# Chunked attention with a Fourier-mix MLP on one core: the first batch's memory values through GpSimd's queue, a negation on VectorE, large loads first, and a cheaper extra row in a newly searched order

## The chip, the cores and the metric

The kernel runs on one core of a Trainium2 chip. A core has five engines that run in parallel, each through its own list of instructions in order: TensorE (PE; its weight loads are PEld), VectorE (DVE), ScalarE (ACT), GpSimd (POOL) and SyncE (SP), which here only issues DMAs. DMAs can be issued from SP, from ACT and from POOL. The metric is the device time of one execution in microseconds, the median over runs.

## The reference

Inputs are float32: q, k and v of 4 batches x 8 heads x 768 positions x 64, eight memory keys and values per head, and two weight matrices of 512 x 2048 and 2048 x 512. Cut to what matters:

```python
for c in range(768 // 32):                        # chunks of 32 queries
    l, r = max(0, 32*c - 16), min(768, 32*c + 40)
    k_full = concat([mem_k, k[:, :, l:r]]);  v_full = concat([mem_v, v[:, :, l:r]])
    a = softmax(q[:, :, 32*c:32*c+32] @ k_full.T / 8)
    out[:, :, 32*c:32*c+32] = a @ v_full
x = out with its heads side by side               # (4, 768, 512)
u = x + real(fft(fft(x, axis=1), axis=2))
un = (u - mean(u)) / sqrt(var(u) + 1e-6)          # over the last axis
result = u + maximum(un @ w_ch1, 0) @ w_ch2
```

## The kernel before

A batch is handled as four pairs of heads; pair n (0 to 15) lives in the buffers `qs`, `ks` (three of each) and `va` (four). For a pair, q and k are loaded as bf16 by GpSimd's queue (L383) and turned on TensorE (`trq`, `trk`, L415; the last batch by DMA instead). The 768 queries are 12 tiles of 64; a tile sees 96 keys: 8 memory keys, 16 to the left, its own 64 and 8 to the right. `va` holds for each tile the values of these 96 keys, with a column of ones beside them that gives the softmax's sum. Scores (`sc`) go through exp on ScalarE (`e`), are multiplied with `va` (`xa` for tiles 0 to 5, `xo` for 6 to 11, L523) and normalised on VectorE into `xsb` (L533, L534).

**Values.** `e_load_v` (L385 to L406) fills `va` from SP: the first tile's own 64 rows for both heads (L399), and then for each head the large load of 80 rows x 11 tiles (`run`, L392), the 8 rows to the right (L392) and the memory values (L405). In the first batch the second head's large load is issued by ScalarE instead (`half == 1`). Before the loads, `e_edges` (L353 to L355) writes the ones and clears the edges, on VectorE for `va0` and on GpSimd for the others; `e_edge_ones` (L360 to L365) corrects the ones at the edges, on GpSimd, and the first `xa` of a pair waits for that too.

**Fourier part.** The two-dimensional transform is done as matrix products with cosine and sine tables made on the chip: the angles on VectorE (L1065 to L1074), the sines on ScalarE (L1228). The first batch also needs negated copies of half of the sequence tables, `odd`, made by `e_negatives` (L1230 to L1232) on GpSimd. In the sequence direction only rows 0 to 384 are computed (`ps`, L729 for batch 0, L595 for the others); the remaining rows follow by mirror symmetry, through a round trip to DRAM (`x_rows`, `x_back`). For batches 1 to 3, `h_columns` (L789) does the same in the feature direction: per block of 128 rows it computes only the independent columns, and `h_copy`, `h_ends` and `h_mix` build the mirrored ones. Row 384 is left over from the three blocks of 128. `e_last_row` (L640 to L647) computes this extra row by six matmuls with one column of weights each, over all 256 columns of both halves (even and odd columns, `par`), into partition 0; `h_last` (L819 to L824) copies it from PSUM with two ScalarE copies, and then GpSimd may add the mirrored rows back (`h_sum_back`, L829). Mean and variance (L841), normalisation, a turn by TensorE (batch 0) or by DMA, and the MLP follow: `ph` (L906), ReLU on ScalarE (L915), then `pc` (L924 as plain products; L973 with seven products of halves for eight, on sums that VectorE makes, L961), added into `xsb` (L978).

**Order.** Nothing is scheduled by the hardware. Every step is a task of a planner (`Plan`) with an engine, an estimated cost, the tasks that it waits for and the buffers that it takes and gives. An order per engine is written out as five lists of task numbers (`lists`); the planner plays them through with its costs, and the instructions are emitted in the order that comes out. In the opening, whenever the planner's model leaves TensorE without work, it puts in dummy matmuls on a tile of zeros (`dz`, `idle`): narrow ones of 128 columns (L1046) up to 7 us of its own clock and wide ones of 512 (L1038) after that, until the first batch's Fourier data is there. They are instructions like any others: they run whether or not the real wait was as long.

A DMA signals its end on a semaphore. Eight are used in turn by the DMAs of SP and ACT, eight others by those of GpSimd, so that an issue can wait for the landing of an earlier one that used the same semaphore.

Of the kernel before, what the change touches and what calls it, by code (L numbers as in the profile page):

```python
# [14 lines left out]
ALU = mybir.AluOpType  # L15
# [193 lines left out]
def kernel(  # L209
# [176 lines left out]
    def e_load_v(n, half=None):  # L386
# [12 lines left out]
        nc.sync.dma_start(v1[OWN:OWN + 64, :, 0, 0:D],  # L399
                          v[b, 2 * pr:2 * pr + 2, 0:64].rearrange("h p d -> p h d"))  # L400
# [239 lines left out]
    def e_last_row(b):  # L640
        pm = pm_of[b, 0] if b < HALVED else pm_of[b, 0].rearrange("p (c j) -> p c j", c=2)
        for par in range(2):
            todo = [(up_of[b, par, ab][0][:, part, HS:HS + 1], (cosD, nsinD)[ab])
                    for ab in range(2 - par) for part in range(2)]
            for i, (lhs, rhs) in enumerate(todo):
                nc.tensor.matmul(pm[0:1, par, :], lhs, rhs[:, par, :], start=(i == 0),
                                 stop=(i == len(todo) - 1))  # L647
# [171 lines left out]
    def h_last(b):  # L819
        pm, full = pm_of.pop((b, 0)), full_of[b, 0][0:1]  # L820
        pl = pm[0:1].rearrange("p (c j) -> p c j", c=2)
        nc.scalar.copy(strided(full, 0, [[HD + 1, 2], [1, HD]]), pl)
        nc.scalar.copy(full[:, HD:HD + 1], pl[:, 0, 0:1])  # L823
        let_go(pm)  # L824
# [262 lines left out]
    t_used, t_val = {}, {}  # L1087

    def attention(n):
# [11 lines left out]
        if first:  # L1101
            if n % 2 == 0:
                for m in (n, n + 1):
# [4 lines left out]
        lv = add("SP", 2.7 if first else 2.5, lambda: e_load_v(n, 0 if first else None),  # L1108
                 [t_edges[n] if n < NV else None, t_used.get(("va", n % NV))] + ([t_lb[2], t_lb[3]] if n == 3 else []),
                 behind=t_x2.get(b - 2) if not first else t_lv[n - 1] if n % 2 else None if n == 0 else t_lb[n + 1],  # L1110
                 take=("va",), moved=1.65 if first else 2.7, grain=0.038, head=0.5 if first else 0.9, late=LATE,
# [44 lines left out]
        for g in range(2):  # L1156
# [39 lines left out]
            v_ = add("PE", 0.79, mode="v", emit=lambda g=g: e_values(n, g), after=[x_, lv, lb, t_ones[n]], take=(tag,),  # L1196
# [33 lines left out]
    def e_negatives():  # L1230
        for i, tab in enumerate((cosS, sinS)):
            nc.gpsimd.tensor_scalar(odd[:, i], tab[:, 1], -1.0, None, ALU.mult)  # L1232
# [24 lines left out]
    t_neg = shared(add("POOL", 3.3, e_negatives, [t_sines], rank=100))  # L1257
# [438 lines left out]
```

## Time and profile before

| what | value |
|---|---|
| time, median of 3 runs | 271.45 us (270.34 to 272.12) |
| profiled execution: span from first to last instruction | 268.6 us |
| median less that span | 2.85 us |
| TensorE busy | 262.2 us, 98% of the span |
| VectorE, ScalarE, GpSimd busy | 203.0, 161.9, 89.6 us |
| `ph` L906, 768 matmuls of 128x256 | 88.9 us |
| DMA moved | 40.00 MB, mean 149 GB/s |

The profile is of one execution. A row of the timeline reads: start, duration, engine, line, operation, output<-inputs, tile, count, and in brackets how long the engine was idle before and what released it; rows of one kind that follow each other are merged. Matmuls overlap in the pipeline, so that the time from one start to the next, and not the duration shown, is what one costs. An engine with a q behind its name is its sequencer, which issues DMAs. The waits list who waited for whom: total, times, longest. The chain of work follows back from the last instruction to what released it at each step; `...` marks lines left out.

### The profile page before, as it was taken

Reading aid. Unit: us, or ns where it says so; the run is one execution under the profiler, and the core shown is the slowest. Engines: PE = TensorE matmul, PEld = TensorE weight load, DVE = VectorE, ACT = ScalarE, POOL = GpSimd, SP = SyncE. Lnnn points to the kernel's source line nnn. Section 1 sums busy time; section 2 is a strip of 40 time slices with the busy share of each in tenths; the row PEclk is TensorE's granted clock in tenths of the full one; section 3 lists DMA queues with packets and bytes.
Section 4 is the critical chain, followed back from the end, with each engine's and each line's share of the span. In section 5 each row is a group of like instructions: output and inputs, shape, how many; then the busy total and the mean of one; then the engine's idle time right before and its main releaser. Section 6 shows DMA issues by size and latency. Waiting matters only on the chain.

```text
span 268.6 us, 8357 instructions
## 1 busy us (share of the span) xinstructions
PE 262.2 (98%) x3469; PEld 216.9 (81%) x3469; DVE 203.0 (76%) x456; ACT 161.9 (60%) x312; POOL 89.6 (33%) x159
## 2 busy tenths in 40 slices
PE   7999999999999999999999999999999999999995
PEld 7566796888855688857798888888988888888884
DVE  6867769853399699999999989999887855344454
ACT  6757879898854478776823884726537171715150
POOL 7985463035120460655460641005006331000000
PEclk9999999999999999999999999999999999999999
DMA  6999999999999999569999944873903233434263
GB/s 105 209 178 201 215 202 207 190 181 194 182 254 178 150 213 164 130 176 212 238 190 175 185 100 76 196 106 58 218 2 82 63 76 79 95 61 103 57 161 97
DMA packets 116118, 40.00 MB, mean 149 GB/s; under 512 B 104560, under 2 KB 111472, under 8 KB 116080
## 3 DMA queue, kind: packets, MB, share of 16 engines
q1 hardware_dynamic: 90304, 22.64, 46.4%
q0 software_dynamic: 21472, 15.21, 35.2%
q10 hardware_dynamic: 4304, 1.62, 2.9%
q8 instruction: 27, 0.44, 0.7%
q14 instruction: 11, 0.09, 0.1%
HBM read 37.36 MB, written 13.37 MB: 189 GB/s over the span
## 4 chain that ended last, share of the span: by engine, by line
PE 82%; DVE 13%; POOL 2%; issue 2%; ACT 0%; POOLq 0%
PE ph L906 27%; PE pc L973 21%; PE pc L924 5%; PE ps L595 5%; PE xa L523 4%; PE xo L523 4%; PE idle L1038 3%; PE ps L729 3%; PE pm L768 2%; PE sc L471 2%; PE trk L415 2%; DVE st L841 1%; DVE xsb L534 1%; PE pm L789 1%; PE trq L415 1%
## 5 line engine op out<-in xcount | busy, mean ns | idle before, releaser
L906 PE MATMUL ph<-unT,w_sb 128*128 128x256 f16 x768 | 88.9, 273 | 0.0
L915 ACT ACTIVATE hT<-ph 128x512 f16<-128x512 f32 x96 | 55.2, 598 | 52.8 <-PE pc L973 37.5
L906 PEld LDWEIGHTS <-w_sb 128*128 128x128 f16 x768 | 74.3, 98 | 9.5 <-issue 0.6
L973 PEld LDWEIGHTS <-hT 128*128 128x128 f16 x360 | 34.6, 98 | 4.6 <-issue 0.4
L973 PE MATMUL pc<-w_sb,hT 128*128 128x256 f16 x288 | 36.6, 273 | 0.0
L978 DVE TENSOR_TENSOR xsb<-pc,xsb 128x256 f32<-128x256 f32 x64 | 26.1, 420 | 13.8 <-PE pc L973 12.8
L829 POOL TENSOR_TENSOR xsb<-mix,xr 128x512 f32<-128x512 f32 x9 | 12.4, 1389 | 45.1 <-ACT mix L823 35.5
L506 ACT ACTIVATE e<-sc,mbias 96x192 f32<-96x192 f32 (+1 forms) x48 | 18.9, 467 | 5.2 <-PE sc L494 5.2
L924 PE MATMUL pc<-w_sb,hT 128*128 128x512 f16 x96 | 21.7, 379 | 0.0
L481 ACT ACTIVATE e<-sc,mbias 96x384 f32<-96x384 f32 x32 | 17.0, 572 | 6.8 <-PE sc L471 6.8
L961 DVE TENSOR_TENSOR S<-hT 128x768 f16<-128x768 f16 (+1 forms) x18 | 7.6, 421 | 17.8 <-ACT hT L915 17.5
L855 ACT ACTIVATE un<-xsb,rs 128x512 f16<-128x512 f32 x18 | 14.4, 820 | 5.3 <-POOL rs L870 5.3
L973 PE MATMUL pc<-w_t,S 128*128 128x256 f16 x144 | 17.4, 273 | 0.0
L924 PEld LDWEIGHTS <-hT 128*128 128x128 f16 x96 | 9.1, 98 | 10.1
L841 DVE BATCH_NORM_STATS2 st<-xsb 128x6 f32<-128x512 f32 x24 | 16.3, 681 | 0.8 <-POOL xsb L829 0.7
L973 PEld LDWEIGHTS <-S 128*128 128x128 f16 x144 | 14.0, 98 | 1.6
L523 PE MATMUL xa<-va,e 96*64 96x65 f32 x384 | 14.7, 226 | 0.0
L523 PEld LDWEIGHTS xa<-va,e 96*64 96x64 f32 x384 | 12.5, 137 | 2.3 <-issue 1.7
L523 PE MATMUL xo<-va,e 96*64 96x65 f32 x384 | 14.1, 223 | 0.0
L1038 PE MATMUL idle<-dz 128*128 128x512 bf16 x46 | 12.9, 387 | 1.0 <-DVE va L353 1.0
L433 ACT COPY qT<-trq 128x768 bf16<-128x768 bf16 x12 | 9.5, 795 | 6.6 <-PE trq L415 6.4
L523 PEld LDWEIGHTS xo<-va,e 96*64 96x64 f32 x384 | 12.6, 138 | 0.4 <-ACT e L481 0.2
(192 smaller groups left out, 491.6 us busy)
## 6 DMA issues: line engine op xcount, KB each, us to landing
va<-in_v_dram SPq DMA_DIRECT2D x28, 220.0 KB
w_sb<-in_moe_w_ch_dram POOLq DMA_DIRECT2D x8, 512.0 KB, 9.3
out_dram<-xsb SPq DMA_DIRECT2D x12, 256.0 KB
qs<-in_q_dram POOLq DMA_DIRECT2D x12, 192.0 KB, 6.9
ks<-in_k_dram POOLq DMA_DIRECT2D x12, 192.0 KB, 6.4
x_rows<-xsb POOLq DMA_DIRECT2D x3, 768.0 KB, 5.1
xr<-x_back POOLq DMA_DIRECT2D x3, 768.0 KB, 5.7
out_rows<-xsb SPq DMA_DIRECT2D x9, 256.0 KB
```

What stands on the lines that cost most here:

```text
L481: nc.scalar.activation(e1[0:KEYS, :, :, ts(half, 32)], sc[0:KEYS, :, 0:6, ts(half, 32)], AFT.Exp, bias=mbias[0:KEYS, half:half + 1], scale ...
L506: nc.scalar.activation(to, src, AFT.Exp, bias=mbias[0:KEYS, half:half + 1], scale=1.0 / math.sqrt(D))
L523: nc.tensor.matmul(xa[64 * half:64 * half + 64, st, hh, 0:65], e1[0:KEYS, hh, t6, :], v1[0:KEYS, hh, 6 * g + t6, 0:65], start=True, stop=True)
L595: nc.tensor.matmul(out_[:, sp, :], part[:, ab, sp * 3 + st, c0:c1], tab[:, sp, st, :], start=(st == 0 and i == 0), stop=(st == 2 and i == 1))
L841: nc.vector.bn_stats(st6, xs[b][:, kt, :])
L855: nc.scalar.activation(un, xs[b][:, kt, :], AFT.Identity, bias=rs[:, 1:2], scale=rs[:, 0:1])
L906: nc.tensor.matmul(ph[:, k, :], w1_sb[:, dt, ts(HH * k + i, P)], unT_of[b, j][:, dt, :], start=(dt == 0), stop=(dt == NDT - 1))
L915: nc.scalar.activation(hT_of[b, j][:, :, i, :], ph, AFT.Relu, bias=0.0, scale=1.0 if (b, j) in FAST else -1.0)
L924: nc.tensor.matmul(pc_of[b, j, r], hT_of[b, j][:, k, i, ts(r, P)], w2_sb[:, HH * k + i, :], start=(i + k == 0), stop=(i + k == HH))
L973: nc.tensor.matmul(pc_of[key], a[:, i, :], w[:, i, :], start=(i == 0 and new), stop=(i == HH - 1), skip_group_check=not new)
L978: nc.vector.tensor_tensor(u, pc, u, ALU.add)
L1038: nc.tensor.matmul(fill_of[0], dz, strided(dz, 0, [[0, 4], [1, P]]), start=True, stop=True)
```

## The change

It has five parts.

1. Memory values of the first batch. A new function `load_mem` issues what L405 issued. For the first batch (`half` not None) it is a task of its own on GpSimd, one per pair and head, eight in all, which both value products of the pair wait for; the other batches issue it from SP as before.
2. Large loads first. `e_load_v` issues the large load of the first head ahead of the first tile's 64 rows.
3. The negation `odd` moves from GpSimd to VectorE.
4. The extra row. Only the independent columns are computed, 129 of the even half and 128 of the odd one; the even half goes to partition 0 and the odd one to partition 32, in turn. `h_last` mirrors the rest, with four copies in place of two.
5. The planner's costs for these steps are changed, and all five lists are new. By them the program has 44 wide dummies where it had 46, and 76 narrow ones where it had 68.

```diff
@@ e_load_v
-        nc.sync.dma_start(v1[OWN:OWN + 64, :, 0, 0:D],
-                          v[b, 2 * pr:2 * pr + 2, 0:64].rearrange("h p d -> p h d"))
         for hh in range(2):
             if half is None or hh == 0:
                 run(OWN - LEFT, LEFT + 64, 1, NT - 1, 64 - LEFT, hh, nc.sync)
+            if hh == 0:
+                nc.sync.dma_start(v1[OWN:OWN + 64, :, 0, 0:D],
+                                  v[b, 2 * pr:2 * pr + 2, 0:64].rearrange("h p d -> p h d"))
             run(OWN + 64, RIGHT, 0, NT - 1, 64, hh, nc.sync)
-            nc.sync.dma_start(v1[MEM0:MEM0 + NMEM, hh, :, 0:D],
-                              mem_v[b, 2 * pr + hh].unsqueeze(1).to_broadcast([NMEM, NT, D]))
+            if half is None:
+                load_mem(n, hh, nc.sync)
+
+    def load_mem(n, hh, by):
+        b, pr = seq[n]
+        by.dma_start(va[n % NV][MEM0:MEM0 + NMEM, hh, :, 0:D],
+                     mem_v[b, 2 * pr + hh].unsqueeze(1).to_broadcast([NMEM, NT, D]))
@@ e_last_row
-        pm = pm_of[b, 0] if b < HALVED else pm_of[b, 0].rearrange("p (c j) -> p c j", c=2)
-        for par in range(2):
-            todo = [(up_of[b, par, ab][0][:, part, HS:HS + 1], (cosD, nsinD)[ab])
-                    for ab in range(2 - par) for part in range(2)]
-            for i, (lhs, rhs) in enumerate(todo):
-                nc.tensor.matmul(pm[0:1, par, :], lhs, rhs[:, par, :], start=(i == 0),
-                                 stop=(i == len(todo) - 1))
+        pm = pm_of[b, 0].rearrange("p (c j) -> p c j", c=2)
+        todo = [(par, ab, part) for ab in range(2) for part in range(2) for par in range(2 - ab)]
+        for par, ab, part in todo:
+            nc.tensor.matmul(pm[32 * par:32 * par + 1, par, 0:NJ - par],
+                             up_of[b, par, ab][0][:, part, HS:HS + 1],
+                             (cosD, nsinD)[ab][:, par, 0:NJ - par], start=(ab, part) == (0, 0),
+                             stop=(ab, part) == (1 - par, 1))
@@ h_last
-        pl = pm[0:1].rearrange("p (c j) -> p c j", c=2)
-        nc.scalar.copy(strided(full, 0, [[HD + 1, 2], [1, HD]]), pl)
-        nc.scalar.copy(full[:, HD:HD + 1], pl[:, 0, 0:1])
+        pl = pm.rearrange("p (c j) -> p c j", c=2)
+        for par, first in ((0, 0), (1, HD + 1)):
+            n, row = NJ - par, pl[32 * par:32 * par + 1, par]
+            nc.scalar.copy(full[:, first:first + n], row[:, 0:n])
+            nc.scalar.copy(strided(full, first + HD - par, [[-1, NJ - 1]]), row[:, 0:NJ - 1])
@@ e_negatives
-            nc.gpsimd.tensor_scalar(odd[:, i], tab[:, 1], -1.0, None, ALU.mult)
+            nc.vector.tensor_scalar(odd[:, i], tab[:, 1], -1.0, None, ALU.mult)
@@ tasks
-    t_neg = shared(add("POOL", 3.3, e_negatives, [t_sines], rank=100))
+    t_neg = shared(add("DVE", 0.5, e_negatives, [t_sines], rank=100))
...
+    for n in range(HP):
+        for hh in range(2):
+            t_mem = add("POOL", 0.66, lambda n=n, hh=hh: load_mem(n, hh, nc.gpsimd), [t_edges[n]],
+                        moved=0.13, grain=0.02, head=1.8)
+            for g in range(2):
+                t_pv[n, g]["after"].append(t_mem)
@@ lists: all five are new; the start of GpSimd's
-            36, 2, 11, 37, 55, 54, 13, 15, 18, 71, 9, 8, 19, 12, 70, 113, 10, 14, 88, 89, 32, 91, 208, 207,
+            2, 36, 37, 13, 55, 19, 54, 1085, 1086, 9, 71, 15, 70, 11, 1087, 18, 1088, 12, 88, 1092, 89, 1091, 8, 10,
+            1090, 1089, 91, 208, 225, 14, 207, 244, 135, 243, 224, 124, 114, 245, 246, 242, 241, 265, 264, 353, 260,
```

In GpSimd's new list (1085 to 1092 are the memory loads, two per pair in the order of the pairs) the iota (2) stands ahead of the first q load (36). The ones of `va0` and `va1` (8, 10) stand behind the fourth pair's q and k loads (88, 89) and memory loads (1092, 1091). On ScalarE the second head's large load of the first pair (38, third in the list before) now stands behind the first sine (105). On VectorE the clearing of `dz` (16) stands behind the edges of `va0` (7), and the negation (113) stands between two normalisations of the first batch. In SP's new list stores of finished rows come later.

More of the change, by code (lines that the diff above doesn't have):

```diff
@@ L1107, in attention @@
             lb = t_lb[n]
-        lv = add("SP", 2.7 if first else 2.5, lambda: e_load_v(n, 0 if first else None),
+        lv = add("SP", 2.1 if first else 2.5, lambda: e_load_v(n, 0 if first else None),
                  [t_edges[n] if n < NV else None, t_used.get(("va", n % NV))] + ([t_lb[2], t_lb[3]] if n == 3 else []),
                  behind=t_x2.get(b - 2) if not first else t_lv[n - 1] if n % 2 else None if n == 0 else t_lb[n + 1],
-                 take=("va",), moved=1.65 if first else 2.7, grain=0.038, head=0.5 if first else 0.9, late=LATE,
+                 take=("va",), moved=1.42 if first else 2.7, grain=0.038, head=0.5 if first else 0.9, late=LATE,
                  dense=0.84, cap=0.67 if first else 1.0)
@@ L1195, in attention @@
                 continue
-            v_ = add("PE", 0.79, mode="v", emit=lambda g=g: e_values(n, g), after=[x_, lv, lb, t_ones[n]], take=(tag,),
+            v_ = t_pv[n, g] = add("PE", 0.79, mode="v", emit=lambda g=g: e_values(n, g), after=[x_, lv, lb, t_ones[n]], take=(tag,),
                      rank=len(plan.tasks) + (50 if (n, g) == (2, 1) else 25) if first else None,
@@ L1392, in columns @@
                 if kt == 3:
[L1393 removed]
+                    cols[kt] = add("PE", 0.36, mode="s", emit=lambda: e_last_row(b), after=[t_sum[0]])
                 return
```

5 lines of the change are left out of this document (2 added, 3 removed), and 108 rows, old and new, of the table lists.

## The prediction

> **What bounds the kernel now.** I read the page first, then the waits of TensorE, then TensorE's timeline of the opening.
>
> ```profile
> span 268.6 us, 8357 instructions
> PE 262.2 (98%) x3469; PEld 216.9 (81%) x3469; DVE 203.0 (76%) x456; ACT 161.9 (60%) x312; POOL 89.6 (33%) x159
> ```
> ```profile
> PE idle L1038 <- DVE va L353: 1.0, 1, 1.0
> PE trq L415 <- DVE ident_b L1013: 0.6, 1, 0.6
> PE ps L595 <- ACT hT L915: 0.5, 1, 0.5
> PE pm L768 <- DVE up L757: 0.5, 1, 0.5
> PE mps L1214 <- DVE mkb L1208: 0.4, 1, 0.4
> ```
>
> TensorE is busy 98% of the span, and these five waits are nearly all that it has. A microsecond is won only where TensorE loses an instruction or a wait. But not all of its work is useful: the opening is padded with dummy matmuls (`idle`), which stand in the program whether or not the data has come.
>
> ```profile
> 1.05 0.61 PE L1038 MATMUL idle<-dz 128*128 128x512 bf16 x1 [1.05 <-DVE va L353]
> 1.45 4.68 PE L1046 MATMUL idle<-dz 128*128 128x128 bf16 x48
> 7.19 1.29 PE L1046 MATMUL idle<-dz 128*128 128x128 bf16 x20
> 8.31 1.46 PE L1038 MATMUL idle<-dz 128*128 128x512 bf16 x6
> 10.21 0.23 PE L1214 MATMUL mps<-ident_b,mkb 128*128 128x128 bf16 x1 [0.44 <-DVE mkb L1208]
> 11.06 1.90 PE L1038 MATMUL idle<-dz 128*128 128x512 bf16 x8
> 12.90 0.35 PE L471 MATMUL sc<-qT,kTb 64*128 64x64 bf16 x12
> 13.18 0.54 PE L415 MATMUL trk<-turn_b,ks 100*64 100x100 bf16 x16
> 13.55 0.51 PE L415 MATMUL trq<-ident_b,qs 96*64 96x96 bf16 x16
> 16.11 0.92 PE L523 MATMUL xa<-va,e 96*64 96x65 f32 x24
> 30.15 0.59 PE L1038 MATMUL idle<-dz 128*128 128x512 bf16 x2
> 42.08 0.39 PE L1038 MATMUL idle<-dz 128*128 128x512 bf16 x1
> ```
>
> From 10.2 us on each start follows the matmul before it without a gap: the opening is as long as its dummies make it. Eight wide ones run from 11.06 to 12.90; less about 0.1 for the change of tile shape that is 0.22 each. A narrow one, once the array is warm, takes (8.31 - 7.19) / 20 = 0.056.
>
> **The opening, walked in the new order.** The changed program has 44 wide dummies for 46 and 76 narrow for 68. The three at 30.15 and 42.08 are gone, and one more stands ahead of the first `xa`. `dz` is now cleared behind three memsets of `va` on VectorE: TensorE starts about 0.45 later, at 1.5, and the first wide dummy ends at 1.9. The first 48 narrow ones take 4.5 as before (4.68 less the last one's tail), 28 more take 1.57: 7.95. Then two wide (8.4), `mps` (8.5), `trq` (8.9), six wide (10.2), `trk` of the second pair and of the first (11.1), eight wide and the change of shape (12.95), `sc` (13.2), `trq` (13.65), seven wide (15.2), `sc` and one wide (15.8): the first `xa` starts at 15.9 instead of 16.11. The waits of 0.6 and 0.4 are what paid for the added dummies; now dummies lie over them. From there to the first Fourier matmul both lists hold 19 wide dummies; after it the new one has none for three, 3 x 0.22 = 0.65. Together -0.85, if every load is there in time.
>
> ```profile
> 1.36 0.88 POOL L383 DMA_DIRECT2D qs<-in_q_dram  x1 [0.87 <-POOLq L1680]
> 8.73 1.33 POOL L362 TENSOR_SCALAR_AFFINE_SELECT va<-va 32x2 f32<-32x2 f32 x1
> 13.54 1.80 POOL L1232 TENSOR_SCALAR odd<-sinS 128x579 f16<-128x579 f16 x1
> ```
> ```profile
> 8.65 0.69 ACT L1228 ACTIVATE sinS<-rS 128x579 f16<-128x579 f32 x1 [0.56 <-DVE rS L1070]
> ```
> ```profile
> 8.62 1.06 SPq L392 DMA_DIRECT2D va<-in_v_dram  x2
> 15.20 0.59 SPq L399 DMA_DIRECT2D va<-in_v_dram  x1
> ```
> ```profile
> L383 POOL DMA_DIRECT2D ks<-in_k_dram x8: 629/642/682, 3.5 to 38.1; - x8
> DMA to landing us min/median/max: 5.1/6.1/10.0
> ```
>
> *Second head of the first pair's values* (ScalarE's queue, L392). It now stands behind the first sine. That sine starts earlier, since the iota no longer waits for the `qs` issue of 0.88: about 7.7. The nearest row for the landing is SP's wait: the large load issued at 8.62 is what the issue at 15.20 waited for, 6.6. So it lands at 14.3, under the 15.9 at which `xa` wants it. Cost nothing; the cover is 1.6.
>
> *Memory values of the first batch* (eight loads, from SP's queue to GpSimd's). On GpSimd each costs an issue; the nearest row is `ks`, 0.64, so 5.1 in all, against the negation's two that leave (1.80 the one shown). Bounds: from nothing, where the engine would wait anyway, to 0.88 each. In the software queue the first pair's two are fifth and sixth, issued at about 6 and landing 6.1 later, at 12.1. But the engine runs in order, and more hangs on it: the fourth pair's `qs` and `ks` issues and its two memory loads, the second of which waits for the first pair's second to land, now stand ahead of the ones of `va0` (L360 to L365), which `xa` needs. 12.1 + 0.65, and 1.4 for ones of which one is stretched to 1.33 again, make 14.1. Cover 1.8: cost nothing. Behind them wait the third pair's memory values, the gate, and the next batch's `ks` and `qs`, all wanted later; one more of the four W1 loads now stands behind GpSimd's Fourier column (L677), and W1 is first read behind all of the first batch's Fourier work. Cost nothing.
>
> *SP's queue.* Five issues a pair in place of seven, large ones first, so the third pair's are less held back than by the wait until 15.20. No matmul waits there today: gain nothing.
>
> ```profile
> DVE zs L533 <- PE xa L523: 2.1, 2, 1.2
> L961 DVE TENSOR_TENSOR hT<-hT,S x9: 672/681/1731, 139.5 to 261.2; 128x1024 f16<-128x1024 f16 x9
> ```
>
> *The negation on VectorE.* Two of 579 f16 elements; from 0.68 for 1024 with two operands, about 0.4 each, and at most the 1.8 of GpSimd. They stand between two normalisations, where VectorE idled up to 1.2 for `xa`: 0.8 fits, cost nothing; without that cover, 0.8.
>
> **The extra row.**
>
> ```profile
> 103.95 0.28 PE L789 MATMUL pm<-cosD,up 128*128 128x129 f16 x2
> 104.06 0.27 PE L789 MATMUL pm<-nsinD,up 128*128 128x128 f16 x2
> 107.46 0.38 PE L646 MATMUL pm<-cosD,up 128*1 128x256 f16 x2
> 108.21 0.52 PE L494 MATMUL sc<-qT,kTb 64*128 64x64 bf16 x24
> ```
> ```profile
> L822 ACT COPY mix<-pm x3: 557/574/574, 108.4 to 200.8; 1x512 f32<-1x512 f32 x3
> L823 ACT COPY mix<-pm x3: 143/143/144, 108.8 to 201.2; 1x1 f32<-1x1 f32 x3
> ```
>
> Six matmuls of 256 columns take 107.46 to 108.21, 0.75: 0.65 and the change of shape. At 129 columns the pitch is 104.06 - 103.95 over two, 0.055; six are 0.33, so 0.43 with the change, -0.32. The two halves go to different 32-column groups of the array in turn, which could overlap. `trk` above does the like: sixteen of 100 columns from 13.18 to 13.55, 0.023 each. Then 0.22 or less is left, -0.43 a row. The Trainium skill (TensorEngine Tiling (Array Packing), Key Properties) says that different tiles run their weight loads and matmuls in parallel; by it the larger gain holds, and the `trk` rows agree. I take -0.32, since the row of equal width has it. ScalarE's two copies (0.71) become four of 128 or 129: at 0.14 + 0.43 x 128 / 512 = 0.25 each, 1.0, +0.3 on ScalarE before GpSimd may sum back; only GpSimd waits for it.
>
> How much counts depends on the place:
>
> ```profile
> 97.03 0.42 DVE unT L883
> ...
> 122.14 0.61 DVE st L841
> ...
> 128.67 3.28 PE ps L595 x36
> ```
>
> In the chain of work, batch 1's row (107.46) lies in a stretch that VectorE sets, from 97 to 128.67: what TensorE wins there becomes wait, so 0. For batches 2 and 3 the chain lies on TensorE: 2 x 0.32 = -0.65.
>
> **The rest of the order.** The four other lists were searched anew; TensorE does the same matmuls in blocks moved by a few microseconds. Nothing in the trace prices this: between -0.55 (the wait at 128.67 goes) and +0.8 (one more stretch like it). I take 0, as the dense stretches hold spare MLP blocks. SP's copies back through DRAM come later, three of batch 3 in a row at the end, but the last store still waits for the last sum.
>
> **Sum.** -0.85 - 0.65 = -1.5 on the span of 268.6: 267.1. The times run from 270.34 to 272.12; the median, 271.45, is 2.85 over this span. Forecast 270.0.
>
> **Rivals.**
> *More is won.* All three rows at -0.43, the wait at 128.67 gone, the opening as above: -0.85 - 1.3 - 0.55 = -2.7, 268.7. For: the `trk` pitch. Against: VectorE's load in 97 to 128.
> *The opening is not shortened.* A load comes 0.85 later than wanted, as dummies in the old program covered waits that the new one shows: 271.45 - 0.65 = 270.8. For: the covers are 1.6 and 1.8, and landings vary from 5.1 to 10.0.
> *GpSimd's queue makes it slower.* The first pair's second memory load takes the 10.0 of the slowest `ks`: landed at 16, then 0.65 for the issue that waits for it and 1.4 for the ones: `xa` at 18.1 instead of 15.9, +2.2, 272.2, slower than now. It decides once the ones end past 15.9, then one for one. Against: the median is 6.1. The Trainium skill (SBUF — State Buffer, SBUF: two separate sides) warns that VectorE can lock GpSimd out of a port while it writes descriptors, 620 ns becoming 3100; by it eight issues would cost 20 us more on GpSimd. The trace does not agree so far: no issue shown took over 0.88 with VectorE busy beside it.
>
> **How the numbers follow.** Forecast 0.45 (its own range 269.2 to 270.6), more won 0.24, opening not shortened 0.20, GpSimd slower 0.11. The measurement tells about 1%: 268.74 and 274.16. Faster: half of "more won" and a little of the forecast, 0.15. Slower: only where GpSimd is late more than once, 0.05. The rest, 0.80, is within 1%. The range runs from 268.1, "more won" with its own spread as the forecast's (0.6), to 272.4, just past the slower case.
>
> **What would show it.** Right: the first `xa` near 15.9 and no new TensorE wait ahead of 30 us; L646's successor at 0.33 or 0.22 a row; a wait before the `ps` near 127 that is no shorter. Wrong: a TensorE wait on a DMA or on GpSimd at the first `xa`, ones of `va0` ending past 15.9, a stretched issue on GpSimd, or VectorE's chain of 97 to 128 longer.

## The result, and the profile after

The changed kernel is slower: 283.76 us median (279.75 to 286.35, 4 runs) against 271.78 (270.34 to 277.40, 4 runs) of the kernel before on the same chip, a ratio of 1.0385, 95% interval 1.0335 to 1.0436. The forecast was 270.0, and 272.4 was the upper end of its range. Part of the runs of both kernels is disturbed (the kernel before then takes 274 to 280) and left out of the ratios, so that a median can lie above what its ratio says; the profiled runs of the changed kernel (284.88), `e_tpool` and `e_row` are among these, and what they show is used below only where other kernels show it too.

The page of the changed kernel, its span and engines, and TensorE's busy tenths, granted clock and DMA in 40 slices of 7.1 us:

```profile
span 283.2 us, 8366 instructions
PE 264.7 (93%) x3475; PEld 218.8 (77%) x3475; DVE 200.3 (71%) x458; ACT 161.9 (57%) x318; POOL 89.1 (31%) x165
...
PE   7959999999999999999998999999999999999940
...
PEclk9995999999999999999999999999999999999995
DMA  6997999999989999979999932913001265547048
```

TensorE's work is nearly the same, 264.7 us for 262.2. The span has 14.6 us more, and they lie at its two ends: the third slice is busy by five tenths and the fourth runs at half the clock, and the last slice and a half have no TensorE work at all, while DMAs still move. Between the ends little changed: from the first Fourier product (`ps`) to the start of the last matmul it is 236.06 us, before 236.02.

**The head.** TensorE's waits:

```profile
PE trk L421 <- ACT qT L439: 3.4, 1, 3.4
PE idle L1046 <- DVE mhalf L331: 1.6, 1, 1.6
PE ph L914 <- DMA unT<-un: 1.0, 1, 1.0
```

Where the longest wait of the kernel before was 1.0, there is one of 3.4 now, of the third pair's `trk` for the copy `qT` on ScalarE. TensorE's timeline and ScalarE's show what that copy stood behind:

```profile
17.01 0.92 PE L529 MATMUL xa<-va,e 96*64 96x65 f32 x24
17.86 0.39 PE L1046 MATMUL idle<-dz 128*128 128x512 bf16 x1
21.62 0.88 PE L421 MATMUL trk<-turn_b,ks 100*64 100x100 bf16 x16 [3.37 <-ACT qT L439]
...
23.83 1.57 PE L529 MATMUL xo<-va,e 96*64 96x65 f32 x24
```
```profile
7.28 0.97 ACTq L392 DMA_DIRECT2D va<-in_v_dram  x2
...
9.56 2.16 ACTq L392 DMA_DIRECT2D va<-in_v_dram  x1
...
20.41 0.32 ACTq L392 DMA_DIRECT2D va<-in_v_dram  x1
20.77 0.80 ACT L439 COPY qT<-trq 128x768 bf16<-128x768 bf16 x1 [4.41 <-DMA va<-in_v_dram]
```

ScalarE runs in order. The fourth pair's large load (20.41) stands ahead of the copy, and it could not be issued, as its semaphore is that of the second pair's large load on ScalarE, issued with the first pair's by the row at 7.28. That one landed only at 20.4, some 12.7 after its issue at 7.7; the prediction had taken 6.6 for such a load. The `xo` at 23.83 then takes 1.57 where it took 0.92. The clock tells why (the columns are the stretch in us, its length, the busy us of PE, PEld, DVE, ACT and POOL with their instructions, the granted clock, the time of the DMA packets as a share of the 16 engines' time, which passes 1 where packets overlap, and GB/s):

```profile
15.00:18.00 3.00, 2.76 (x44) 1.61 (x42) 1.20 (x2) 1.35 (x4) 1.43 (x7) 1.00 1.35 195
18.00:21.60 3.60, 0.25 (x1) 0.11 (x1) 0.15 (x1) 0.83 (x2) 0.39 (x1) 0.88 1.40 160
21.60:25.00 3.40, 3.38 (x52) 2.33 (x53) 1.92 (x3) 1.96 (x4) 0.00 (x0) 0.50 1.22 128
25.00:28.60 3.60, 3.60 (x64) 2.19 (x60) 1.38 (x5) 1.27 (x3) 1.18 (x3) 0.65 0.22 41
```

After TensorE has stood, its clock is at half speed: 3.4 x 0.50 + 3.6 x 0.35 = 3.0 us of work are lost behind the 3.4 of standing. The first `xa` is 0.9 later than before instead of the forecast 0.2 earlier, and the first `ps` comes at 35.91 instead of 29.13.

**The tail.** SP's waits, and its timeline at the end:

```profile
SPq L995 <- DMA out_dram<-xsb: 12.4, 2, 12.2
```
```profile
260.55 0.33 SPq L998 DMA_DIRECT2D out_rows<-xsb  x1
273.07 0.88 SPq L995 DMA_DIRECT2D out_dram<-xsb  x2
...
276.79 1.79 SPq L1005 DMA_DIRECT2D out_dram<-out_rows  x2
278.63 1.36 SPq L991 DMA_DIRECT2D out_dram<-xsb  x1
```

SP stood from 260.9 to 273.1 ahead of a store of rows that had long been finished. It uses again the semaphore of a ScalarE store of the last batch, which could be issued only when its sums were there, at 270.99, and landed at 273.05. Four copies (two of them in the row at 276.79) and the last store queue behind it, and the span ends 11.2 us behind the start of the last matmul; before it was 3.5.

**The extra row**, in the timeline of batch 1:

```profile
114.06 0.28 PE L650 MATMUL pm<-cosD,up 128*1 128x129 f16 x4
114.17 0.28 PE L650 MATMUL pm<-nsinD,up 128*1 128x129 f16 x2
114.38 0.52 PE L500 MATMUL sc<-qT,kTb 64*128 64x64 bf16 x24
```

From its start to the next block it is 0.32 now and was 0.75: 0.43 less a row, the larger of the two sizes that the prediction gave.

### The profile page after: what moved, and what is told of

It reads as the page before. It is cut to its first block, busy times and chain, and to the rows that moved or that the text cites. A ratio compares the mean times of both kernels' runs of the same rounds, so it can differ in the third digit from the quotient of the medians.

```text
span 283.2 us, 8366 instructions
## 1 busy us (share of the span) xinstructions
PE 264.7 (93%) x3475; PEld 218.8 (77%) x3475; DVE 200.3 (71%) x458; ACT 161.9 (57%) x318; POOL 89.1 (31%) x165
## 3 DMA queue, kind: packets, MB, share of 16 engines
q10 hardware_dynamic: 4304, 1.62, 3.3%
## 4 chain that ended last, share of the span: by engine, by line
PE 80%; DMA 7%; DVE 4%; POOL 2%; ACT 2%; issue 1%; ACTq 0%; POOLq 0%
PE ph L914 29%; PE pc L981 17%; PE pc L932 7%; PE ps L601 5%; DMA va<-in_v_dram 4%; PE xa L529 4%; PE xo L529 4%; DMA unT<-un 3%; PE ps L735 3%; PE idle L1046 2%; PE pm L774 2%; PE trq L421 1%; PE sc L477 1%; PE trk L421 1%; PE pm L795 1%; PE sc L500 1%
## 5 line engine op out<-in xcount | busy, mean ns | idle before, releaser
L969 DVE TENSOR_TENSOR S<-hT 128x768 f16<-128x768 f16 (+1 forms) x18 | 8.3, 463 | 20.3 <-ACT hT L923 20.2
L863 ACT ACTIVATE un<-xsb,rs 128x512 f16<-128x512 f32 x18 | 14.1, 811 | 3.9 <-POOL rs L878 3.9
L529 PE MATMUL xo<-va,e 96*64 96x65 f32 x384 | 14.8, 229 | 0.0
L613 ACT CAST up<-ps 128x386 f16<-128x386 f32 x12 | 7.2, 602 | 11.3 <-PE ps L601 11.2
```

Of the source, the lines that this page charges most:

```text
L529: nc.tensor.matmul(xa[64 * half:64 * half + 64, st, hh, 0:65], e1[0:KEYS, hh, t6, :], v1[0:KEYS, hh, 6 * g + t6, 0:65], start=True, stop=True)
L863: nc.scalar.activation(un, xs[b][:, kt, :], AFT.Identity, bias=rs[:, 1:2], scale=rs[:, 0:1])
```

## The experiments

All of them, in one table. First `ps` and last matmul are starts in the profiled run, whose span is beside them; ratios are to the kernel before, run on the same chip.

| kernel | median us (lowest to highest, runs) | ratio, 95% interval | first `ps` | last matmul | span |
|---|---|---|---|---|---|
| before | 271.78 (270.34 to 277.40, 4) | | 29.13 | 265.15 | 268.6 |
| after | 283.76 (279.75 to 286.35, 4) | 1.0385, 1.0335 to 1.0436 | 35.91 | 271.97 | 283.2 |
| e_tpool | 277.43 (275.12 to 280.12, 4) | 1.0135, 1.0056 to 1.0214 | 38.24 | 274.46 | 278.4 |
| e_sp | 278.82 (274.95 to 283.13, 4) | 1.0168, 1.0075 to 1.0261 | 32.77 | 267.30 | 273.2 |
| e_sp_in_before | 284.54 (283.95 to 285.07, 4) | 1.0471, 1.0397 to 1.0545 | 29.25 | 272.03 | 283.1 |
| e_act | 281.83 (280.61 to 284.19, 6) | 1.0351, 1.0288 to 1.0415 | 34.82 | 271.30 | 282.5 |
| e_act_tpool | 274.51 (271.94 to 277.05, 10) | 1.0102, 1.0055 to 1.0149 | 31.85 | 266.95 | 270.9 |
| e_warm | 273.42 (273.26 to 273.60, 4) | 1.0097, 1.0082 to 1.0112 | 31.96 | 267.60 | 271.6 |
| e_early_tpool | 273.87 (273.75 to 275.58, 4) | 1.0130, 1.0093 to 1.0168 | 32.74 | 268.07 | 272.0 |
| e_all | 273.75 (272.06 to 275.15, 4) | 1.0109, 1.0057 to 1.0160 | 32.56 | 268.71 | 272.7 |
| e_nomem | 272.42 (271.53 to 274.57, 4) | 1.0072, 1.0021 to 1.0123 | 30.03 | 266.04 | 269.8 |
| e_best | 272.46 (271.27 to 278.48, 10) | 1.0040, 0.9993 to 1.0087 | 29.42 | 267.06 | 270.9 |
| e_late | 274.56 (272.50 to 277.56, 4) | 1.0114, 1.0069 to 1.0158 | 29.20 | 268.99 | 272.4 |
| e_mem | 278.04 (276.70 to 279.12, 4) | 1.0280, 1.0226 to 1.0333 | 31.91 | 271.84 | 275.3 |
| e_rest | 275.77 (274.64 to 276.30, 4) | 1.0178, 1.0149 to 1.0207 | 30.03 | 270.90 | 274.4 |
| e_neg | 276.22 (273.77 to 278.48, 4) | 1.0137, 0.9989 to 1.0285 | 29.13 | 270.53 | 274.0 |
| e_big | 270.34 (270.30 to 273.99, 10) | 0.9976, 0.9927 to 1.0026 | 29.12 | 265.15 | 268.6 |
| e_row | 273.35 (269.50 to 278.44, 12) | 0.9962, 0.9912 to 1.0012 | 30.69 | 273.29 | 276.7 |
| e_memfirst | 275.55 (270.52 to 280.69, 12) | 0.9987, 0.9930 to 1.0044 | 29.13 | 266.52 | 270.0 |
| e_row_big | 269.55 (269.54 to 270.07, 8) | 0.9947, 0.9922 to 0.9971 | 29.12 | 264.91 | 268.4 |

### The tail

The theory was that both losses come from the turn of the eight semaphores that SP and ScalarE share. The rival for the tail: SP's stores simply come too late in its list, whoever issues the others. `e_tpool` leaves SP's list and moves the last batch's direct stores to another queue, with semaphores of its own:

```diff
 def e_out_half(b, st, half):
-    (nc.sync, nc.scalar)[half].dma_start(out[b, ts(st, P), ts(half, HD)],
+    (nc.sync, nc.gpsimd)[half].dma_start(out[b, ts(st, P), ts(half, HD)],
 def e_out(b, st):
-    (nc.scalar if b == B - 1 else nc.sync).dma_start(out[b, ts(st, P), :], xs[b][:, st, :])
+    (nc.gpsimd if b == B - 1 else nc.sync).dma_start(out[b, ts(st, P), :], xs[b][:, st, :])
```

> The changed kernel, with the last batch's three direct stores issued by GpSimd, which is idle there, instead of by ScalarE; SP's list and order stay. Theory (SP's late store of an earlier batch uses again a semaphore of ScalarE's last stores): SP no longer stands from 260.9 to 273.1, only the copies that wait for the last sums follow the last matmul, and the span ends some 3 us behind TensorE as before the change: 6 to 8 us less, 273 to 276. Rival (SP's later order of stores is itself too late, whoever issues the others): 0 to 2 us less, 279 to 282.

The ratio fell from 1.0385 to 1.0135, about 6.8 us (4.6 to 8.9 by the interval of the second). SP's timeline:

```profile
263.03 0.33 SPq L998 DMA_DIRECT2D out_rows<-xsb  x1
263.40 0.93 SPq L995 DMA_DIRECT2D out_dram<-xsb  x2
...
275.22 0.34 SPq L991 DMA_DIRECT2D out_dram<-xsb  x1
```

The store that stood for 12 us follows its neighbour at once, in the same place of the same list, and the span ends 3.9 behind the last matmul's start. The rival falls: not the place of the store but the semaphore made it late.

`e_sp` gives the changed kernel the SP list of the kernel before, `e_sp_in_before` gives the kernel before the new SP list and nothing else.

> The changed kernel with SP's list of the kernel before; the other four lists stay. Theory: the tail is as before the change, 6 to 8 us less: 273 to 276; the opening keeps its wait of 3.4 us. Rival (the end is late because the last sums are late, not because of SP): no gain, 280 to 283.

> The kernel before with SP's list of the changed kernel, the other lists and all code as before. Theory (SP's new list alone makes the late end, by its late store that uses again a semaphore of ScalarE's last stores): SP stands some 12 us ahead of that store, the span ends 10 to 11 us behind the last matmul instead of 3.5, 276 to 280. Rival (the tail is late only together with the other new lists): 270.3 to 272.

With the old list the span ends 5.9 us behind the last matmul's start, the tail is mostly undone (1.0168); the new list alone makes the kernel before at least about as slow as the whole change does (1.0471, with an interval that overlaps that of 1.0385). Its SP waits and the end of its SP timeline repeat those above:

```profile
SPq L987 <- DMA out_dram<-xsb: 17.5, 3, 12.3
```
```profile
266.75 1.30 SPq L990 DMA_DIRECT2D out_rows<-xsb  x1
273.13 0.87 SPq L987 DMA_DIRECT2D out_dram<-xsb  x2
```

The span ends 11.1 behind the last matmul's start. The rest of its loss is a stand of 4.3 us of a value product for its memory values at 31 us, and the half clock behind it; why SP's list, which differs up to there only in the order of three later pairs' loads, brings that about was not found. In the changed kernel the old list also gave back what the extra rows and the three dummies less win: from first `ps` to last matmul `e_sp` has 234.53 us, 1.5 less than the 236.06 of the changed kernel.

### The head: semaphore, standing, clock

The rivals here: the large loads are late in themselves, as they share the DMA engines, and the wait only names one of them; or the new order of the compute engines loses the time. `e_act` takes the load that could not be issued out from ahead of the copy; no other instruction moves, the dummies included, though the turn of the semaphores shifts for the next loads (73 is the load, 51 the exp of the second pair):

```diff
-        for t in plan.settled(lists):
+        todo = plan.settled(lists)
+        moved(todo, 73, 51)
+        for t in todo:
             t["emit"]()
```

> The changed kernel, with one issue moved: the fourth pair's second large value load stands behind the second q copy and the second exp on ScalarE instead of ahead of them; the matmuls, the dummies and all other lists stay. Theory (a DMA semaphore used again blocks ScalarE): the wait of 3.4 us of TensorE for the q copy goes, and with it the slow clock behind it; first Fourier product near 31 us instead of 36; time 4 to 6 us less than the changed kernel's 279.8 to 282.7, so 275 to 277. Rival (the large loads themselves come late, as they share the DMA engines): the second pair's load lands near 20.4 all the same, its value product waits for it, and at most 2 us are won: 278 to 281. Rival (the searched order of the compute engines is what loses): no gain, 280 to 283.

The wait for the copy was gone (`trk` at 16.81), but the time was not: 1.0351, its interval on that of the changed kernel. TensorE's timeline shows why:

```profile
15.64 0.92 PE L529 MATMUL xa<-va,e 96*64 96x65 f32 x24
...
22.54 0.85 PE L529 MATMUL xo<-va,e 96*64 96x65 f32 x21
25.52 0.48 PE L529 MATMUL xo<-va,e 96*64 96x65 f32 x3 [2.13 <-issue]
```

TensorE stood 2.13 us inside a block of 24 matmuls whose data was all there, behind the 21st, and the half clock followed. "issue" is a wait for nothing that the profile names. In `e_all` below the same place stood 1.75, until 26.05, and the DMA view of 23.3 to 25.0, just ahead of this stand and into it, has a packet of 16 KB of instructions among the loads:

```profile
q1 hardware_dynamic: 589, 0.14, 56.4%
...
q8 instruction: 1, 0.02, 5.2%
```

The four kernels that stood there agree: such a packet ended 1.2 to 1.5 us before the block went on (in `e_act` at 24.07, and the block went on at 25.52), and in `e_nomem` below, which did not stand, it had ended at 19.12, 3.8 ahead of the block's start. So TensorE's own code most likely came late, through the same DMA engines as the loads; that was not tried apart. The theory of the semaphore had named the wait rightly and not the loss: with this wait gone another took its place. `e_act_tpool` has both edits.

> The changed kernel with both: the load moved on ScalarE and the last three stores by GpSimd. Theory (both losses come from semaphores used again, and add up): 10 to 13 us less than the changed kernel, 268 to 271.5, level with the kernel before or up to 2 us faster. Rival (other parts of the change cost too, above all GpSimd's issues): 273 to 277.

1.0102: most of the loss is explained, but not all; the stand within `xo` was still there (1.85).

`e_warm` keeps all of `e_tpool` and adds useless work, 12 wide dummies where TensorE stood:

```diff
+        at = [t.get("no") for t in todo].index(78)
+        todo[at:at] = [dict(emit=plan.fill)] * 12
```

> The changed kernel with the last stores by GpSimd (275.1 to 280.1), and with 12 more wide dummy matmuls (12 x 0.22 = 2.6 us) ahead of the third pair's k products, where TensorE stood 3.4 to 5.1 us. Theory (TensorE's standing halves its clock for 3.4 or 6.8 us behind it): no slice of the clock under full speed, the stretch that took 0.50 a score block is back at 0.35, 1.7 to 3.4 less: 272 to 275. Rival (the low clock has another cause, or the wait alone costs): 275 to 280, the dip stays.

```profile
16.17 0.96 PE L529 MATMUL xa<-va,e 96*64 96x65 f32 x24
17.07 2.98 PE L1046 MATMUL idle<-dz 128*128 128x512 bf16 x13
20.18 0.54 PE L421 MATMUL trk<-turn_b,ks 100*64 100x100 bf16 x16
...
21.48 0.92 PE L529 MATMUL xo<-va,e 96*64 96x65 f32 x24
```

With 2.6 us more work the kernel took 273.26 to 273.60 in all four runs, where `e_tpool` took 275.12 or more; by the ratios, 1.0097 and 1.0135, whose intervals overlap, it is at least no slower, and it is steadier. The mean clock over the span is 0.982 to 0.988 in the four runs of `e_tpool` and 0.999 to 1.000 in those of `e_warm`, and `xo` takes 0.92 again. In `e_tpool`'s profiled run TensorE stood 5.1 us there, and the clock behind that was this:

```profile
24.40:27.80 3.40, 3.37 (x52) 2.32 (x53) 1.92 (x3) 1.96 (x4) 1.41 (x3) 0.50 0.38 85
27.80:31.00 3.20, 3.20 (x64) 1.93 (x60) 1.45 (x6) 1.19 (x3) 1.70 (x6) 0.79 1.05 145
```

So the clock falls because TensorE stands. How long it must stand isn't a fixed number here: over the twenty profiles the clock fell behind three of ten stands of 1.4 to 2.0 us and seven of eight longer ones. `e_best` fell to half behind 1.40; a row of its TensorE and the stretch behind it:

```profile
32.54 0.80 PE L528 MATMUL xa<-va,e 96*64 96x65 f32 x20 [1.40 <-DMA va<-in_mem_v_dram]
```
```profile
34.40:37.80 3.40, 3.40 (x52) 2.94 (x51) 2.14 (x6) 1.68 (x5) 3.26 (x10) 0.57 1.01 199
```

`e_late` (below) kept its clock behind 2.97; its wait, and the stretch behind it:

```profile
PE xa L523 <- DMA va<-in_mem_v_dram: 3.0, 1, 3.0
```
```profile
34.00:37.40 3.40, 3.07 (x61) 2.81 (x62) 2.00 (x6) 1.09 (x4) 3.12 (x10) 1.00 1.20 195
```

The Trainium skill (TensorE: Matmul & The Clock Gate, Part 1: The HAM clock gate) says that TensorE's clock is halved after at least one idle window of about 3.4 us, that the windows run freely, and that it is full again after a busy one. The runs agree on the half, and a window that runs freely would explain why 1.40 can be too long and 2.97 short enough; that a whole window must be idle they do not bear out.

### The head: why the loads are late

The theory: the first pair's second large load, issued at 7.3 instead of 2.2, takes 220 KB out of a quiet stretch into the crowded one. `e_early_tpool` puts it back to the front of ScalarE's list (`moved(todo, 38, 3)`) on top of `e_tpool`; `e_all` adds the edit of `e_act`; `e_late` is the reverse, the kernel before with that load behind the first sine (`moved(todo, 38, 105)`).

> The changed kernel with the last three stores by GpSimd, and with the second head's large load of the first pair back at the front of ScalarE's list (issued near 3 us instead of 7.3); all else stays. Theory (crowding: that load moves 220 KB out of idle DMA time into the stretch from 7 us on, where the queue of SP and ScalarE moved only 0.28 MB in 7 us, so that every later load lands up to 5.5 us later): the second pair's load lands some 5 us sooner, ScalarE no longer stands for its semaphore, the wait of TensorE for the q copy falls under 0.5, the first Fourier product comes at 29 to 31 us, 269 to 272 in all. Rival (the loads are late because of the memory values and the later q and k issues in GpSimd's queue): the wait stays at 2 to 5 us, 275 to 280.

> The same, and the fourth pair's second large load behind the second exp on ScalarE. By the crowding theory this adds little to the kernel above, 269 to 271.5; if the loads stay late, the wait goes to TensorE by another way, as in the kernel where this load alone was moved: 272 to 275.

> The kernel before with one issue moved: the second head's large load of the first pair stands behind the first sine on ScalarE, as in the changed kernel (issue near 8 us instead of 2.2). Theory (crowding): the later loads land later, TensorE waits 1 to 3 us ahead of 30 us, and may lose 1.7 or 3.4 more to the clock: 272 to 277. Rival (it costs nothing, as the prediction had it): 270.3 to 271.5.

`e_late` costs: 1.0114, and its only new wait is the 3.0 shown, not of the first pair but of the fourth pair's value product for its memory values, at 31 us. The reverse is not so clear: in `e_early_tpool` the wait for the copy was 1.0 and the clock stayed full, but neither 1.0130 nor `e_all`'s 1.0109 can be told from `e_tpool`'s 1.0135 (1.0056 to 1.0214). The stand within `xo` (1.7 and 1.8) and waits for `ks` of the second pair (0.7 and 1.2) had taken its place. The expectation of 269 to 272 was missed: the load's place is one cause and, as far as these runs tell, not the main one. The expectation also took the 0.28 MB of one queue for those of SP and ScalarE together. The DMA view of 7 to 14 us has two, q1 with 0.28 MB and q10, whose 1.62 MB over the span are what ScalarE issued, with 0.34; the kernel before has 0.33 and 0.32 there, so this view doesn't show that their traffic was crowded out.

`e_nomem` has the memory values issued by SP again, on top of `e_early_tpool`. `e_mem` is the kernel before with part 1 of the change alone: the eight loads by GpSimd, two of them behind the second pair's q load (54), two behind the clearing of a key buffer (19), four behind the fourth pair's k load (89).

```diff
+        for n, hh, no in ((0, 1, 54), (0, 0, 54), (1, 1, 19), (1, 0, 19), (3, 1, 89), (3, 0, 89), (2, 1, 89), (2, 0, 89)):
+            todo.insert(1 + [t.get("no") for t in todo].index(no),
+                        dict(emit=lambda n=n, hh=hh: load_mem(n, hh, nc.gpsimd)))
```

> The changed kernel with the last stores by GpSimd and the first pair's large load early (273.8, first Fourier product at 32.7), and besides with the first batch's memory values issued by SP again, seven loads a pair. Theory (GpSimd's eight issues and its fuller queue hold back the q and k loads and the code of TensorE): the wait for ks (0.7) goes, the matmuls' stop within xo (1.7) goes or shrinks, first Fourier product at 29.5 to 31, 270 to 272. Rival (what is left of the loss lies in the compute engines' new order and the later start): 273 to 274.5.

> The kernel before, with the memory values of the first batch by GpSimd's queue and nothing else changed; dummies and other lists stay, SP issues five loads a pair. Rival (GpSimd's issues, 0.64 each, and its full queue are what costs): the ones of the first pairs or the later q and k loads are late, a new wait of TensorE ahead of 30 us, 273 to 276. Theory (crowding and semaphores in the new order, not the queue of the memory values): 270.5 to 272, as before.

`e_nomem`: 1.0072, the stand within `xo` gone, the first `ps` at 30.03. `e_mem` was the clearest miss: I expected it level, and it is at 1.0280. Its waits:

```profile
PE xa L528 <- DMA va<-in_mem_v_dram: 2.2, 1, 2.2
PE trk L420 <- DMA ks<-in_k_dram: 1.8, 1, 1.8
```

The 1.8 is for the fourth pair's `ks`, which GpSimd issued at 19.07 instead of 17.41 and which landed 9.4 later instead of 5.6. The 2.2 lies at 61 to 63 us, in the second batch, whose values come by SP as before, and the half clock came behind it; that the delay of the opening had moved on to the next batch's loads is a reading, not shown. So the prediction's rival, GpSimd's queue, is real, though not at the place that it named.

`e_rest` has the two parts left over, the negation on VectorE and the large load first, in the kernel before; `e_neg` and `e_big` have one each. The large load is moved as in the change's first hunk, the negation so (113 is its task, 92 a normalisation):

```diff
-            nc.gpsimd.tensor_scalar(odd[:, i], tab[:, 1], -1.0, None, ALU.mult)
+            nc.vector.tensor_scalar(odd[:, i], tab[:, 1], -1.0, None, ALU.mult)
+        moved(todo, 113, 92)
```

> The kernel before with the two parts that the prediction had at nothing beside the memory values: the negation on VectorE and the large load first in each pair; lists and dummies as before otherwise. The prediction's steps: 0 each, 270.3 to 271.5. Rival (the changed order of loads lets semaphores fall on other loads and holds an issue up): a new wait of TensorE ahead of 30 us, 272 or more.

> The kernel before with the negation on VectorE alone. The prediction's step: two of 0.31 each (by the changed kernel's trace) in place of GpSimd's 1.80 and more, cost nothing: 270.3 to 271.5. Rival (GpSimd, freed of 3.5 us, issues its next q and k loads sooner and crowds the queue of SP and ScalarE; the fourth pair's product waits for its last load): 273 or more.

> The kernel before with the large load first in each pair alone. The prediction's step: nothing, 270.3 to 271.5. Rival (it is this part that gave the 275.8 of the kernel with both): a wait of the fourth pair's value product for its last load, 273 or more.

`e_rest` lost 1.78%. `e_big` costs nothing: 0.9976, and eight of its ten runs lie within 270.30 to 270.57. `e_neg` took 273.77 to 278.48; its interval touches 1, but none of its runs and of `e_rest`'s came under 273.77. The negation itself takes 0.31 each on VectorE and nothing waits for it. GpSimd's timeline tells what happens, here the fourth pair's q and k loads, in `e_neg` and then before:

```profile
13.96 0.65 POOL L383 DMA_DIRECT2D qs<-in_q_dram  x1
14.60 0.63 POOL L383 DMA_DIRECT2D ks<-in_k_dram  x1
```
```profile
16.71 0.70 POOL L383 DMA_DIRECT2D qs<-in_q_dram  x1 [0.18 <-PE xa L523]
17.41 0.63 POOL L383 DMA_DIRECT2D ks<-in_k_dram  x1
```

And TensorE's waits of `e_neg`:

```profile
PE xa L523 <- DMA va<-in_mem_v_dram: 3.7, 1, 3.7
```

GpSimd, freed of 3.5 us of work, issues the two loads 2.8 sooner, and the fourth pair's values, in another queue, land too late. By this reading the slow negation had been holding the loads apart; no run holds the loads back by other means, so it is argued and not shown.

The same wait of the fourth pair's product follows each of these edits (3.0 in `e_late`, 3.7 in `e_neg`, 1.9 in `e_rest`), and it stands, 3.4 long, in the profiled run of `e_row` below, which moves no load. These values seem to have hardly any cover in the kernel before, and four runs each can't tell what a part costs from how much more often it lets this wait appear.

### What is left, and a version that beats both

`e_row` is the kernel before with part 4 of the change alone (`e_last_row`, `h_last`); `e_memfirst` is `e_row` with the first batch's memory values issued by SP ahead of the pair's other loads, by two calls moved up within `e_load_v`; `e_best` is the changed kernel without four parts held to cost (SP's list as before, memory values by SP, the early load, the last stores by GpSimd).

> The kernel before with the new extra row and its copies alone, no list changed. By the changed kernel's trace (0.32 a row instead of 0.75) 0.43 less in each of three rows, 1.3 in all where TensorE sets the pace: 270.0; 270.4 if batch 1's row only becomes a wait. Rival (ScalarE's four copies in place of two hold GpSimd and then the next steps, and eat the gain): 271.3 or more.

> The kernel before with the new extra row, and with the first batch's memory values issued by SP ahead of the pair's other loads instead of behind them; lists as before. Theory (the queue of SP and ScalarE hands out its loads nearly in the order of their issue, and the fourth pair's memory values were the last to land before a value product): the wait of the fourth pair's product for its memory values does not appear, 269.3 to 270.3 in nearly every run. Rival (the shifted turn of the semaphores holds another issue up): 272 or more.

> The changed kernel without the four things found to cost: SP's list as before, memory values by SP, the first pair's large load early, and the last stores by GpSimd. If SP's new list is also what ate the gain of the extra rows (its turned tiles came 1.0 to 1.8 late; with the old list the stretch from the first Fourier product to the last matmul took 234.5 instead of 236.1): 1.5 less than 271.5, so 269.5 to 271. Rival (the new order of the compute engines ate it): 271 to 273.

`e_row`'s lowest time is 269.50 (reached within 0.03 by four runs of twelve), and that of the kernel before beside it 270.30, 0.8 more; the ratio, 0.9962, can't be told from 1. `e_memfirst` failed: its times spread as those of the kernel before do, and in its profile a value product waits 1.5 for another of the loads (`va<-in_v_dram`). The order within a pair only decides which load is the last. `e_best` at 1.0040 is not told from the kernel before either: it keeps a wait of 1.4 for memory values, and the clock behind it.

`e_row_big` is the last: the kernel before with the two parts that cost nothing alone, the extra row and the large load first.

> The kernel before with the two parts of the change that cost nothing when alone: the extra row with its copies, and the large load first in each pair. If both hold together: 270.3 less 0.43 for each of two or three rows, 269.0 to 269.6, and faster than both kernels. Rival (the gain stays within what the loads of the opening take back): 270 to 272.

It is the fastest, 0.9947 (0.9922 to 0.9971) of the kernel before, and its eight runs lie within 269.54 to 270.07. From lowest to lowest it is 0.8 us (269.54 for 270.34), two rows of 0.43.

## Why the prediction was wrong

- *The opening, walked in the new order* is the step that failed, in its condition "if every load is there in time". `e_act`, whose TensorE list is that of the changed kernel, has the first `xa` at 15.64, and 15.9 was forecast; but in the changed kernel's own run it came at 17.01. Of these 1.4 us 1.1 come from the narrow dummies of the start, which wait for no load; the first row is the changed kernel's, the second that of `e_act`:

```profile
1.97 6.83 PE L1054 MATMUL idle<-dz 128*128 128x128 bf16 x76
1.97 5.77 PE L1054 MATMUL idle<-dz 128*128 128x128 bf16 x76
```

TensorE's first narrow dummies follow each other by 0.095, the later ones by 0.056, and how many are slow differs from run to run: 48 in the changed kernel's profile, 27 in `e_act`'s, 22 to 49 over the twenty. The walk took the 4.5 for its first 48 from one run. In the kernel before, the waits of 0.6 and 0.4 take such differences up: in eight of the ten profiles with its TensorE list the first `xa` stands at 16.08 to 16.11, with 22 to 47 slow ones. With dummies laid over these waits, the difference goes through to the first `xa`. After it the third pair's `trk` stood 3.4, and the half clock, which the prediction did not price at all, took 3.0 more. The forecast's -0.2 at the first `ps` became +6.8 in the profiled run.

- *Second head of the first pair's values*: forecast to land at 14.3, cover 1.6, cost nothing. It was still in time for the first `xa` at 17.01, but landed only near 16.6, 9.3 after its issue, when SP, whose next issue uses its semaphore, went on; moved alone it costs 1.14% (`e_late`). The error was to take 6.6 us from one row as the load's own time. It depends on what stands in the queue: the next one took 12.7.
- *Memory values on GpSimd*: cost 0.61 each (0.64 forecast), with the ones of `va0` done at 15.3 (14.1 forecast) and still in time, and yet cost 2.8% alone, it seems by the later loads that they hold up. The forecast's cover looked at the first pair only.
- *SP's queue*, "gain nothing", missed what five loads a pair instead of seven do in a new order: the eight semaphores fall on other pairs of DMAs, and one of these fell across ScalarE's copy.
- *Negation on VectorE*: 0.31 each (0.4 forecast), hidden as forecast, and yet 1.4% slower alone, with an interval that touches 1, probably since GpSimd's loads then come sooner. "Cost nothing" was right for the engine and, if so, wrong for the transfers that it sets off.
- *Extra row*: right in mechanism, the larger size holds, 0.43. Two rows that count are 0.86, and `e_row_big` has 0.8. The larger size, which the prediction worked out beside the Trainium skill (TensorEngine Tiling (Array Packing), Key Properties), was the better one.
- *Rest of the order*, forecast at 0 with "the last store still waits for the last sum": this is the second step that failed, and the larger, about 6.8 us. The sentence is true, and the other direction was overlooked: an older store of SP came to wait for the last sums too, by ScalarE's semaphore.
- Of the rivals, "GpSimd's queue makes it slower" had the right sign, 0.11 chance, and a price of 2.2; the case that happened, a wait that halves the clock behind it and a store that stands for the last sums, was not among them.

Open: why SP's new list alone makes the fourth pair's product wait (`e_sp_in_before`), whether the stand within `xo` is the late code, and how much the negation costs; the parts' costs, each measured alone, also add up to more than the whole change, as they all act on the same few covers.

## What to carry to other kernels

Price a moved load, or an issuing engine made faster, by all transfers that share its DMA engines, and not by its own landing time: in a crowded opening every cover is common, and the row that shows 6.6 us can become 12.7. When DMAs of two engines take semaphores in turn, look which earlier DMA each issue of a new order waits for; an old store can end up behind the last sum, and an in-order engine behind a load that it does not need. Where TensorE stands for 2 us or more, count the half clock behind it, and consider filling the wait: with twelve useless matmuls the kernel was no slower here, and steadier. A walk from one profile carries the slow start of that one run with it; a wait that takes up such differences is not all loss.

## What the runs showed of the hardware

- TensorE's clock fell to 0.50 for 3.4 or 6.8 us behind ten stands of 1.40 to 5.07 us, and stayed full behind seven of 1.46 to 1.85 and one of 2.97.
- TensorE's first narrow matmuls followed each other by 0.095 instead of 0.056, until 3.7 to 7.1 us, by the run.
- A block of 24 matmuls whose data was there stopped for 1.7 to 2.1 us within, at the same place in four kernels, with a 16 KB instruction packet that ended 1.2 to 1.5 us before the block went on.
- Six matmuls with one column of weights, in turn in two 32-column groups, took 0.32 us to the next block, with the change of shape in it; one after the other they would have taken 0.43 by an estimate (6 x 0.055 and 0.10).
- A 220 KB load took 6.6 us in one opening, and two took 9.3 and 12.7 in the other, with eight large loads of values among the traffic of both.
